# Attention and an MLP in one Trainium2 kernel: every piece of work placed anew, matmuls on zeros in TensorE's early gaps, the last rows copied out in halves

## The chip, the cores and the metric

The kernel runs on one core of a Trainium2 chip. A core has TensorE (PE: matmuls; PEld in the profile is the part of it that loads weights), VectorE (DVE), ScalarE (ACT), GpSimd (POOL) and SyncE (SP), which here issues the DMAs. The metric is the device time of one execution in microseconds, as a median of several. Times below are us unless marked ns.

## The reference, cut to what matters

```python
# q, k, v: (4, 8, 768, 64) f32; n_global 8, n_local 96; w_in (512, 2048), w_out (2048, 512) f32
scores = q @ k^T / sqrt(64)
rel = pos[:, None] - pos[None, :]
keep = (pos[None, :] < n_global) | ((rel >= 0) & (rel < n_local))
scores = scores - slopes * dist            # per head, dist from rel
a = softmax(where(keep, scores, -1e9))
x = (a @ v) rearranged to (3072, 512)      # 4 batches x 768 tokens, 8 heads x 64
h = x @ w_in
g = where(h >= 1, h, where(h <= -1, 0, (h + 1)**2 / 4))
out = g @ w_out                            # (3072, 512) f32
```

## The kernel before

The 3072 tokens are cut into 24 units of 128 rows (4 batches with 6 row blocks each). In a unit, each row block needs the few global keys and the keys of its own block and the one before it, 256 columns, so attention is eight heads of 128 by 256. Two units make a chunk of 256 tokens, on which the two products of the MLP run: 12 chunks, c = 0 to 11. The products come in f16 as three matmuls each: an operand is split into a high part (names with h: `qh`, `kh`, `xh`, `wih`, `woh`, `gh`) and a low one (the rest after the high part: `xh`'s second half, `wil`, `wol`, `gl`).

A unit u has two halves (heads 0 to 3 and 4 to 7; names such as `s12_0`) and passes through this chain:

- `scores` on PE into `s` (24 matmuls), `masked` on DVE into `z`, the exponential on ACT;
- `split_p`: ACT writes the high part of `ph`, DVE the low part;
- `turn_p`: SP issues a DMA transpose `pt<-ph`;
- `attend` on PE into `av` (24 matmuls), `scale_x` on DVE into `x`;
- `split_x`: ACT writes the high part of `xh`; the low part is written by the engine that the constant `XL` names, "p" for POOL, "v" for DVE;
- `turn_x`: SP issues a DMA transpose `xt<-xh`.

Once both units of a chunk are there, the first product `ffn1(c, g)` takes 8 groups g of 24 matmuls into a tile `h` (`h4_7` is group 7 of chunk 4), `gelu` takes five steps on ACT, DVE and POOL that end in `gh` (ACT) and `gl` (POOL), and the second product `ffn2(c, t, f)` collects 48 matmuls for each of the chunk's two row blocks t in a PSUM tile `o` (`o11_1`). `finish` scales `o` into `ob` on ACT and SP sends it out. The first units (block 0 of each batch) go a separate f32 way (`first_load` and on, with transposes `tp` and `xtp` on PE). The weights come in 32 pieces, which DVE turns to f32 (`w_bits`, last step `w_f`), ACT and POOL split (`w_hi`, `w_lo`); `check_load` and `check_reduce` read the weights once more for a range check.

What sets the order: every piece of work is a call that `at(t, f, ...)` puts into a list with a planned time. The list is sorted and numbered, and the table `PLACE` then names the numbers in the order in which the calls are made. Each engine runs its instructions in that order, and SP issues the DMAs in that order. A number that `PLACE` doesn't name is not called. `spare(0)` is a PSUM tile of the pool `ps_o` that nothing reads, and `warm(n)` runs n matmuls of a 128x128 tile of zeros into it. Before, 32 such matmuls run: 8 ahead of the first scores (from `WARM`), and groups of `WA` = 3 among the first units' work.

Of the kernel before, what the change touches and what calls it, by code (L numbers as in the profile page):

```python
# [17 lines left out]
P = 128  # L18
# [38 lines left out]
XL = "p"  # L57
# [6 lines left out]
FLOAD = [-0.95, -0.52, 15.64, 24.01]  # L64
VLOAD = [-4.77, 11.54, 18.15, 28.68]
FIRST = [4.37, 7.29, 10.29, 15.54, 26.68, 37.85, 48.2, 54.41]
WARM = [(1.0, 8)]
WLOAD = [0.8, 1.0, 8.0]
WA = 3
# [3 lines left out]
TAB = -0.77  # L73
TBC = -1.99
RC = 52.97
E3 = [-19.46, -14.0, -6.17, -0.47, 3.78, 8.46, 16.26, 20.67]
PER = 47.0
SOFF = -13.94
FETCH = 16.26
CONV = 9.6  # L80
KG = 3.41
CHK = 7.39
VCONV = 10.53
VFETCH = 8.71
AVL = 14.35
GEL = [2.7, 3.48, 4.59, 5.91, 5.91]
CK0 = 199.09
CK1 = 573.64
CKL = 10.36
WO = [2.79, 3.98, 5.09]  # L90
FO = [0.26, 1.06, 2.5, 3.37, 3.48, 4.67, 5.72, 6.5, 6.59, 7.54]
UO = [0.55, 1.5, 4.0, 5.66, 6.33, 1.69, 1.96, 3.06, 3.38, 3.41]
BO = [1.94, 2.51]
SO = [0.63, 0.65, 2.38, 1.0]
# [4 lines left out]
WG = 3.75  # L99
PB = 2.64  # L100
NCH = NU // 2
WLAG = 5.0
PLACE = [
# [139 lines left out]
]  # L243


@with_exitstack
def attention_then_moe(ctx, tc, q, k, v, n_global, n_local, w_in, w_out, out):
# [950 lines left out]
```

## Time and profile before

| | |
|---|---|
| median of 3 executions | 638.66 us (638.55 to 640.11) |
| profiled execution | 637.52 us, of which the span of instructions is 635.7 us |
| busy share of the span | PE 96%, DVE 70%, PEld 66%, ACT 65%, POOL 47% |
| mean granted TensorE clock | 0.98 of full speed |
| matmuls and weight loads | 5588 each |

The span runs from the first to the last instruction; the profiled execution's time is 1.82 us more. The median lies 1.14 us above the profiled execution. Names in a row such as `pt<-ph` are output and input. An idle time in brackets stands before an instruction, with what ended it.

### The profile page before, as it was taken

To read this page: it belongs to the slowest core of one execution; us is meant where nothing else is said; L and a number is where in the kernel's file an instruction comes from. 1 tells how busy PE (TensorE), PEld (TensorE's weight loads), DVE (VectorE), ACT (ScalarE), POOL (GpSimd) and SP (SyncE) were. 2 spreads that over 40 slices of the span, in tenths; PEclk is the share of its full clock that TensorE was granted. 3 is DMA by queue.
4 is the path that set the end of the run, shared out by engine and by line. 5 is a ranking of instruction groups with operands and counts; after the bars stand their busy time and mean duration, and the time that the engine had idled before them with its cause. 6 is when DMAs were issued, how large, how long until landed. Compare 5 with 4: busy or idle time off the path is not lost.

```text
span 635.7 us, 14747 instructions
## 1 busy us (share of the span) xinstructions
PE 607.6 (96%) x5588; PEld 417.1 (66%) x5588; DVE 442.2 (70%) x1109; ACT 412.1 (65%) x1070; POOL 296.8 (47%) x266
## 2 busy tenths in 40 slices
PE   7888799999999999999999999999999999999996
PEld 4666575656876766767767667666666766766652
DVE  6999999977956676776776776776677686533420
ACT  4868898998867665775785775676585674432220
POOL 0336785775563543563653563463554533322210
PEclk8889899999999999999999999999999999999999
DMA  6748586578944565556555555766554643531001
GB/s 201 250 147 247 182 252 197 125 134 191 168 93 75 109 154 141 154 146 163 144 139 135 158 135 144 171 143 139 127 165 110 140 133 78 125 116 35 1 34 39
DMA packets 144084, 88.08 MB, mean 139 GB/s; under 512 B 108165, under 2 KB 124549, under 8 KB 144005
## 3 DMA queue, kind: packets, MB, share of 16 engines
q1 hardware_dynamic: 144000, 87.05, 54.1%
q8 instruction: 46, 0.75, 0.5%
q14 instruction: 34, 0.27, 0.1%
q10 hardware_dynamic: 4, 0.00, 0.0%
HBM read 54.53 MB, written 6.29 MB: 96 GB/s over the span
## 4 chain that ended last, share of the span: by engine, by line
issue 31%; POOL 26%; PE 25%; DVE 9%; ACT 5%; DMA 2%; POOLq 0%; SPq 0%; ACTq 0%; DVEq 0%
PE o L913 13%; POOL gl L901 11%; PE h L870 8%; POOL xh L801 8%; POOL kh L698 2%; POOL kr L697 2%; DVE w_f L475 2%; POOL qh L698 2%; ACT z L578 1%; POOL qr L697 1%; DMA w_raw<-in_moe_w_out_dram 1%; PE av L785 1%; POOL wol L502 1%; DVE u L893 1%; PE s L742 1%
## 5 line engine op out<-in xcount | busy, mean ns | idle before, releaser
L870 PE MATMUL h<-xt,wih 128*128 128x256 f16 x1536 | 259.7, 274 | 0.7 <-DVE u L893 0.7
L901 POOL TENSOR_TENSOR gl<-u,gh 128x512 f16<-128x512 f32 x96 | 117.8, 1227 | 214.2 <-ACT gh L897 205.2
L870 PE MATMUL h<-xt,wil 128*128 128x256 f16 x768 | 210.8, 274 | 0.0
L870 PEld LDWEIGHTS <-wih 128*128 128x128 f16 x1536 | 149.4, 99 | 32.2 <-DVE u L893 1.6
L888 DVE SCALAR_TENSOR_TENSOR h<-h,u 128x512 f32<-128x512 f32 x96 | 66.7, 695 | 116.3 <-ACT u L883 115.5
L913 PE MATMUL o<-wol,gh 128*128 128x512 f16 x384 | 145.9, 380 | 1.7 <-POOL wol L502 1.7
L913 PE MATMUL o<-woh,gh 128*128 128x512 f16 x384 | 146.4, 381 | 0.0
L913 PE MATMUL o<-woh,gl 128*128 128x512 f16 x384 | 145.8, 380 | 0.0
L883 ACT ACTIVATE u<-h,half 128x512 f32<-128x512 f32 x96 | 65.4, 682 | 87.8 <-PE h L870 87.8
L913 PEld LDWEIGHTS <-gh 128*128 128x128 f16 x768 | 71.5, 98 | 67.2 <-issue 0.5
L578 ACT ACTIVATE z<-z,nm 128x256 f32<-128x256 f32 (+1 forms) x192 | 91.8, 479 | 28.0 <-DVE nm L566 27.5
L897 ACT ACTIVATE gh<-u 128x512 f16<-128x512 f32 x96 | 59.8, 623 | 51.1 <-DVE u L893 51.1
L566 DVE CUSTOM_DVE_ANT_0 z<-s,bias 128x256 f32<-128x256 f32 (+1 forms) x192 | 67.1, 397 | 22.2 <-PE s L742 20.4
L870 PEld LDWEIGHTS <-wil 128*128 128x128 f16 x768 | 75.6, 98 | 9.1
L913 PEld LDWEIGHTS <-gl 128*128 128x128 f16 x384 | 37.7, 98 | 47.7 <-issue 2.9
L760 DVE SCALAR_TENSOR_TENSOR ph<-z,ph 128x1024 f16<-128x1024 f32 x40 | 61.6, 1540 | 9.6 <-ACT ph L758 9.4
L801 POOL TENSOR_TENSOR xh<-x,xh 128x256 f16<-128x256 f32 x40 | 62.2, 1554 | 10.4 <-ACT xh L799 8.8
L893 DVE SCALAR_TENSOR_TENSOR u<-u,h 128x512 f32<-128x512 f32 x96 | 65.4, 681 | 1.4
L534 DVE TENSOR_REDUCE sq<-c_raw 128x1 f32<-128x256 f32 x128 | 49.1, 409 | 0.0
L785 PEld LDWEIGHTS <-pt 128*128 128x128 f16 x960 | 32.8, 98 | 14.5 <-DMA pt<-ph 7.1
L758 ACT ACTIVATE ph<-z 128x1024 f16<-128x1024 f32 x40 | 41.7, 1043 | 0.1
L785 PE MATMUL av<-vh,pt 128*128 128x64 f16 x960 | 34.6, 193 | 4.5 <-DMA pt<-ph 4.3
(100 smaller groups left out, 671.8 us busy)
## 6 DMA issues: line engine op xcount, KB each, us to landing
w_raw<-in_moe_w_in_dram SPq DMA_DIRECT2D x16, 512.0 KB, 4.0
w_raw<-in_moe_w_out_dram SPq DMA_DIRECT2D x16, 512.0 KB, 3.8
c_raw<-in_moe_w_in_dram SPq DMA_DIRECT2D x32, 256.0 KB, 3.5
c_raw<-in_moe_w_out_dram SPq DMA_DIRECT2D x32, 256.0 KB, 3.3
vr<-in_v_dram SPq DMA_DIRECT2D x28, 256.0 KB, 3.9
kr<-in_k_dram SPq DMA_DIRECT2D x28, 256.0 KB, 3.6
qr<-in_q_dram SPq DMA_DIRECT2D x24, 256.0 KB, 4.3
out_dram<-ob SPq DMA_DIRECT2D x24, 256.0 KB, 2.8
```

What stands on the lines that cost most here:

```text
L566: nc.vector.tensor_tensor_reduce(out=p32[u, hf][:, hh, :], in0=pts[u, hf][hh // 2][:, hh % 2, 0:n], in1=bias[:, 4 * hf + hh, base : base + n],
L578: nc.scalar.activation(z, z, AF.Exp, bias=nm[:, c : c + 1], scale=-1.0, accum_out=sums[:, c : c + 1])
L760: nc.vector.scalar_tensor_tensor(phs[u, hf][:, 1, :], zf, SP_, phs[u, hf][:, 0, :], op0=ALU.mult, op1=ALU.subtract)
L785: nc.tensor.matmul(av[:, hh, :], pt[:, a, hh, kt, :], vt[:, c, h * D : (h + 1) * D], start=(n == 0), stop=(n == 5),)
L801: (nc.gpsimd if XL == "p" else nc.vector).tensor_sub(xhs[u, hf][:, 1, :], xs[u, hf], xhs[u, hf][:, 0, :])
L870: nc.tensor.matmul(hp[:, e, :], w[:, dc, f], xt[:, hf, 2 * a + j, :], start=(n == 0), stop=(n == 3 * NDC - 1),)
L883: nc.scalar.activation(us[c, g], hs[c, g], AF.Relu, bias=half, scale=2.0 / (SV * SW), accum_out=su[:, col : col + 1])
L888: nc.vector.scalar_tensor_tensor(ws[c, g], hs[c, g], 4.0 / (SV * SW), us[c, g], op0=ALU.mult, op1=ALU.max)
L893: nc.vector.scalar_tensor_tensor(dst, us[c, g], 4.0, ws[c, g], op0=ALU.min, op1=ALU.mult)
L897: nc.scalar.activation(gh, ws[c, g], AF.Copy)
L901: (nc.gpsimd if GL == "p" else nc.vector).tensor_sub(gl, ws[c, g], gt[c, g][0])
L913: nc.tensor.matmul(po, a[:, cs], w[:, f, :], start=(f == 0 and n == 0), stop=(f == NFC - 1 and n == 2))
```

## The change

The edit has four parts.

1. The planned times (`FLOAD` to `WLAG`, some 30 numbers) and the table `PLACE` are replaced: all work stands in a new order.
2. `XL` goes from "p" to "v": the low part of `xh` moves from POOL to DVE, 40 instructions.
3. 150 calls of `filler` (one matmul on zeros) are listed; `PLACE` names those that are run. `WARM` is empty and `WA` is 1. In all 109 matmuls on zeros are run in place of 32, the last ahead of the first matmul of the second product (`o0`).
4. In the last chunk all 48 matmuls of `o11_0` come ahead of the 48 of `o11_1` (before, they alternate). The last row block is copied out in two halves of 256 columns, the first by ACT and the second by DVE, and is sent in two DMAs, the first issued by SP, the second by ACT.

`TPO` is 0, so the lines with it change nothing.

```diff
-XL = "p"
+XL = "v"
-WARM = [(1.0, 8)]
+WARM = []
-WA = 3
+WA = 1
-AVL = 14.35
+AVL = 12.92
-PLACE = [
-    5, 0, 1, 2, 11, 3, 6, 4, 7, 9, 12, 38, 68, 20, 8, 10, 13, 151, 14, 15, 16, 17, 18, 19, 21, 22, 25, 23, 24,
...
+    3, 0, 1, 2, 5, 7, 8, 71, 9, 4, 72, 11, 73, 74, 37, 6, 231, 300, 75, 10, 12, 13, 14, 19, 15, 16, 17, 18, 20,
...
+NFILL = 150
+TAIL = 1
+TPO = 0
...
+    def filler():
+        warm(1)
...
         for e in range(parts):
             cs = slice(e * n, (e + 1) * n)
-            nc.scalar.activation(ob[:, cs], os_[c, t][:, cs], AF.Copy, scale=1.0 / (SG * SW))
-        nc.sync.dma_start(out[r0 : r0 + P, :], ob)
+            if e:
+                nc.vector.tensor_scalar(ob[:, cs], os_[c, t][:, cs], 1.0 / (SG * SW), None, op0=ALU.mult)
+            else:
+                nc.scalar.activation(ob[:, cs], os_[c, t][:, cs], AF.Copy, scale=1.0 / (SG * SW))
+        for e in range(parts):
+            cs = slice(e * n, (e + 1) * n)
+            (nc.scalar if e else nc.sync).dma_start(out[r0 : r0 + P, cs], ob[:, cs])
...
-                at(t + 0.2, finish, c, x, 1)
+                at(t + 0.2, finish, c, x, 2 if TAIL and c + 1 == NCH and x else 1)
...
-            put_ffn2(c, (0, 1), g, t - (PER / 16 - 0.1 if g and c + 1 < NCH else 0.0))
+            if TAIL and c + 1 == NCH:
+                put_ffn2(c, (0,), g, t0 + 1.3 * g)
+                put_ffn2(c, (1,), g, t0 + 10.5 + 1.3 * g)
+            else:
+                put_ffn2(c, (0, 1), g, t - (PER / 16 - 0.1 if g and c + 1 < NCH else 0.0))
...
+    for n in range(NFILL):
+        at(12.0, filler)
```

Three places show what the table does. The first is SP's order where unit 11 ends and unit 12 begins (`xt5` is the transposed x of chunk 5, `xh11_1` the second half of unit 11, `pt12_0` and `ph12_0` the first half of unit 12, `ob3` the output of chunk 3). Before:

```order
L529 DMA c4_1_raw_3921<-in_moe_w_in_dram 128x2x256
L676 DMA kr14_1_3928<-in_k_dram 128x512
L676 DMA qr14_1_3958<-in_q_dram 128x512
L529 DMA c5_0_raw_4045<-in_moe_w_in_dram 128x2x256
L809 DMA_TRANSPOSE xt5_3520<-xh11_1_4041 128x4x128
L767 DMA_TRANSPOSE pt12_0_4059<-ph12_0_4033 128x16x128
L928 DMA out_0_dram<-ob3_0_4069 128x512
L928 DMA out_0_dram<-ob3_1_4098 128x512
```

And with the change:

```order
L948 DMA out_0_dram<-ob3_0_4023 128x512
L948 DMA out_0_dram<-ob3_1_4055 128x512
L691 DMA kr14_0_4086<-in_k_dram 128x512
L691 DMA kr14_1_4094<-in_k_dram 128x512
L691 DMA qr14_1_4097<-in_q_dram 128x512
L782 DMA_TRANSPOSE pt12_0_4143<-ph12_0_4099 128x16x128
L824 DMA_TRANSPOSE xt5_3618<-xh11_1_4154 128x4x128
L782 DMA_TRANSPOSE pt12_1_4315<-ph12_1_4273 128x16x128
```

The transpose of `ph12_0` stood behind that of `xh11_1` and now stands ahead of it; the two writes of `ob3` stood behind it and now stand further ahead.

The second is where the low part of `xh11_1` is made. Before, on POOL, among the `gl` of chunk 4:

```order
L801 TENSOR_TENSOR xh11_0_3857<-x11_0_3850,xh11_0_3857 128x256
L901 TENSOR_TENSOR gl4_4_3915<-u4_4_3873,gh4_4_3913 128x512
L901 TENSOR_TENSOR gl4_5_4036<-u4_5_3926,gh4_5_4003 128x512
L801 TENSOR_TENSOR xh11_1_4041<-x11_1_4038,xh11_1_4041 128x256
L901 TENSOR_TENSOR gl4_6_4106<-u4_6_4053,gh4_6_4101 128x512
```

With the change, on DVE, behind the low part of `ph12_0`:

```order
L775 SCALAR_TENSOR_TENSOR ph12_0_4099<-z12_0_4052,ph12_0_4099 128x1024
L903 SCALAR_TENSOR_TENSOR h4_7_4059<-h4_7_4059,u4_7_4129 128x512
L642 TENSOR_TENSOR x11_1_4148<-av11_1_4104,r11_1_3924 128x256
L908 SCALAR_TENSOR_TENSOR u4_7_4129<-u4_7_4129,h4_7_4059 128x512
L742 COPY vh11_3_3425<-vg1_2755 32x1024
L816 TENSOR_TENSOR xh11_1_4154<-x11_1_4148,xh11_1_4154 128x256
```

The instruction has left POOL's queue and stands in DVE's, five places behind `ph12_0`'s.

The work that PE does between the scores `s12_0` and the product `av12_0` of the same half is changed too. Before: 9 matmuls of `o3`, `av11_1`, the group `h4_6`, 12 of `o3`, `h4_7`, `s12_1`, 3 of `o4`. Now: `h4_7`, `av11_1`, 24 of `o4`, `s12_1`, 6 of `o4`.

The third is the start of PE's program (`pps` and `pps_n` are two small products on the bias, `zeros` and `spare0` the matmuls on zeros, `s0_0` the first scores). Before, `pps_n` stands behind the last of the first 8 matmuls on zeros:

```order
L434 LDWEIGHTS zeros_122
L434 MATMUL spare0_148<-zeros_122 128x512
L385 MATMUL pps_n_173<-nlow_168,bias_120 128x2
L555 MATMUL s0_0_0_184<-kr0_144,qr0_146 128x128
L555 MATMUL s0_0_1_185<-kr0_144,qr0_146 128x128
```

With the change it stands ahead of the first of six:

```order
L378 MATMUL pps_135<-bias_120 128x1
L394 MATMUL pps_n_155<-nlow_150,bias_120 128x2
L443 LDWEIGHTS zeros_122
L443 MATMUL spare0_162<-zeros_122 128x512
L443 LDWEIGHTS zeros_122
```

Behind these six, single matmuls on zeros and blocks of 7 or 8 of them stand between the products of the first units, for instance 7 ahead of `av0_1` and 8 behind `av3_1`. DVE's order in the first 110 us is changed as well: two more 128x512 steps of the first chunk's gelu (`h1_4`, `u1_4`) stand ahead of the last weight's `w31_f`.

## Rows read from the trace of the kernel before

**Rows 1.** Busy windows: length, then PE, PEld, DVE, ACT, POOL; granted clock, DMA share, GB/s.
```profile
12.00:78.00 66.00, 55.26 (x363) 41.40 (x362) 62.56 (x166) 53.12 (x144) 32.78 (x31) 0.83 0.62 196
78.00:124.00 46.00, 43.73 (x380) 29.89 (x379) 45.10 (x92) 41.76 (x101) 32.91 (x30) 1.00 0.65 186
...
10.10:20.40 10.30, 10.25 (x48) 7.56 (x49) 8.51 (x37) 8.09 (x30) 2.31 (x2) 0.50 0.52 169
```

**Rows 2.** Tile pt from 200 to 550: who waits for it, and issue to landing.
```profile
  PEld L785: 7.1, 6
  PE av L785: 4.3, 5
...
DMA to landing us min/median/max: 4.3/4.3/6.1
```

**Rows 3.** The chain of waits, one chunk's steps: start, length, engine, tile, line, count.
```profile
544.58 0.78 PE s L742 x24
...
547.41 0.70 PE av L785 x24
548.11 2.62 PE h L870 x24
550.73 2.59 PE o L913 x12
```

**Rows 4.** Timeline of unit 10, first half: start, length.
```profile
220.51 1.85 POOL L801 TENSOR_TENSOR xh<-x,xh 128x256 f16<-128x256 f32 x1
...
220.62 1.20 DVE L760 SCALAR_TENSOR_TENSOR ph<-z,ph 128x1024 f16<-128x1024 f32 x1
...
222.39 1.20 SPq L809 DMA_TRANSPOSE xt<-xh  x1
...
223.69 2.07 SPq L767 DMA_TRANSPOSE pt<-ph  x1
...
229.60 0.87 PE L785 MATMUL av<-vh,pt 128*128 128x64 f16 x24 [1.41 <-DMA pt<-ph]
```

**Rows 5.** Timeline of unit 14, first half.
```profile
313.74 0.42 DVE L566 CUSTOM_DVE_ANT_0 z<-s,bias 128x256 f32<-128x256 f32 x1
...
317.79 1.34 DVE L760 SCALAR_TENSOR_TENSOR ph<-z,ph 128x1024 f16<-128x1024 f32 x1 [0.38 <-ACT ph L758]
...
319.19 2.01 SPq L767 DMA_TRANSPOSE pt<-ph  x1
```

**Rows 6.** Lines from 200 to 550: count, busy, mean ns, idle before and its releaser.
```profile
L627 DVE TENSOR_TENSOR x<-av,r 128x256 f32<-128x256 f32 x29 | 12.2, 422 | 2.7 <-PE av L785 2.1
...
L801 POOL TENSOR_TENSOR xh<-x,xh 128x256 f16<-128x256 f32 x29 | 49.4, 1703 | 1.3
```

**Rows 7.** Timelines of DVE and POOL where unit 11's ph is split.
```profile
232.91 2.04 DVE L760 SCALAR_TENSOR_TENSOR ph<-z,ph 128x1024 f16<-128x1024 f32 x1
...
232.72 1.15 POOL L901 TENSOR_TENSOR gl<-u,gh 128x512 f16<-128x512 f32 x1
```

**Rows 8.** Waits from 0 to 12 (us, times, longest), and PE's timeline there.
```profile
DVE nval L386 <- PE pps_n L385: 2.1, 1, 2.1
...
2.92 3.60 PE L434 MATMUL spare<-zeros 128*128 128x512 f16 x8
```

**Rows 9.** Timelines from the last weight to the end of the first `o`.
```profile
115.98 0.68 DVE L475 SCALAR_TENSOR_TENSOR w_f<-w_raw,w_bits 128x512 int32<-128x512 int32 x1
...
118.88 1.15 POOL L502 TENSOR_TENSOR wol<-w_f,woh 128x512 f16<-128x512 f32 x1
...
121.93 0.38 PE L913 MATMUL o<-woh,gh 128*128 128x512 f16 x1
...
123.22 0.38 PE L870 MATMUL h<-xt,wih 128*128 128x256 f16 x2
```

**Rows 10.** The end: ACT's copies and SP's issues of the last two output blocks.
```profile
628.91 1.25 ACT L927 ACTIVATE ob<-o 128x512 f32<-128x512 f32 x2 [17.10 <-PE o L913]
...
629.53 0.98 SPq L928 DMA_DIRECT2D out_dram<-ob  x2
```

More of the change, by code (lines that the diff above doesn't have):

```diff
@@ L62 @@
 FQ = {"k": "sync", "q": "sync", "v": "sync"}
-FLOAD = [-0.95, -0.52, 15.64, 24.01]
-VLOAD = [-4.77, 11.54, 18.15, 28.68]
-FIRST = [4.37, 7.29, 10.29, 15.54, 26.68, 37.85, 48.2, 54.41]
-WARM = [(1.0, 8)]
+FLOAD = [-0.64, 0.7, 15.12, 24.29]
+VLOAD = [-4.85, 13.77, 17.59, 34.66]
+FIRST = [4.37, 6.83, 10.29, 15.54, 27.12, 37.85, 47.39, 54.1]
+WARM = []
 WLOAD = [0.8, 1.0, 8.0]
-WA = 3
+WA = 1
 T0 = 24.5
@@ L72 @@
 GB = 5.42
[L73 to L76, printed above, removed]
+TAB = -1.61
+TBC = -0.92
+RC = 51.6
+E3 = [-19.46, -14.0, -9.93, -2.34, 1.91, 6.59, 14.07, 20.27]
 PER = 47.0
[L78 to L84, printed above, removed]
-AVL = 14.35
[L86 to L94, printed above, removed]
+SOFF = -3.14
+FETCH = 17.57
+CONV = 7.82
+KG = 0.65
+CHK = 6.28
+VCONV = 8.11
+VFETCH = 8.85
+AVL = 12.92
+GEL = [2.85, 3.46, 3.99, 6.47, 7.12]
+CK0 = 299.8
+CK1 = 602.24
+CKL = 8.3
+WO = [2.79, 4.31, 6.34]
+FO = [0.65, 1.06, 2.46, 3.92, 3.63, 4.69, 5.48, 6.52, 6.61, 6.89]
+UO = [0.55, 1.5, 3.54, 5.66, 7.51, 2.65, 3.43, 3.92, 3.99, 4.75]
+BO = [1.13, 2.63]
+SO = [0.72, 0.29, 2.59, 1.22]
 WS = "d"
@@ L98 @@
 PA = 2.76
-WG = 3.75
-PB = 2.64
+WG = 4.92
+PB = 2.85
 NCH = NU // 2
-WLAG = 5.0
+WLAG = 6.03
 PLACE = [
[139 rows of a table removed]
-]
[145 rows of a table added]
+]
+NFILL = 150
+TAIL = 1
+TPO = 0
 @with_exitstack
@@ L461, in w_bits @@
         if s == 0:
-            if num < NFC and num % 2:
+            if num < NFC and num % 2 and not TPO:
                 wbits[n] = spare(1).bitcast(I32).rearrange("p (a b) -> p a b", a=NDC)
@@ L598, in first_turn @@
         whole(u, hf)
-        tp = ps_h.tile([P, 4, P], F32, tag="h", name=f"tp{u}_{hf}")
+        if TPO and u >= TPO:
+            tp = spare(1).rearrange("p (a b) -> p a b", a=4)
+        else:
+            tp = ps_h.tile([P, 4, P], F32, tag="h", name=f"tp{u}_{hf}")
         for hh in range(4):
@@ L991, in fast_path @@
             t = t0 + PER * g / 8
-            put_ffn2(c, (0, 1), g, t - (PER / 16 - 0.1 if g and c + 1 < NCH else 0.0))
+            if TAIL and c + 1 == NCH:
+                put_ffn2(c, (0,), g, t0 + 1.3 * g)
+                put_ffn2(c, (1,), g, t0 + 10.5 + 1.3 * g)
+            else:
+                put_ffn2(c, (0, 1), g, t - (PER / 16 - 0.1 if g and c + 1 < NCH else 0.0))
             if c + 1 < NCH:
```

282 rows, old and new, of the table PLACE are left out of this document.

## The prediction

> **What bounds the kernel now.** I read the windows first, then the chain of waits, then the tile view of `pt` and the timelines behind its waits. In the windows the reader is to see two regimes. From 12 to 78 us DVE is busy 62.56 of 66.00 us and from 78 to 124 45.10 of 46.00, PE 55.26 and 43.73 [rows 1]: the conversion of the weights on DVE sets the pace. PE stands idle there for 10.74 us, and its clock is below full speed too: the mean over 12 to 78 is 0.83, and from 10.1 to 20.4 it is 0.50 [rows 1], the 1.2 GHz level. By that mean 66.00 x 0.17 = 11.2 us of PE's time are lost to the clock. From 124 on PE never stops but for short waits, so there only its waits and its own work count. The chain shows what that work is made of: 24 matmuls of `h` 2.62, 12 of `o` 2.59 (0.216 each), a half's scores 0.78, its `av` 0.70 [rows 3].
>
> The tile view of `pt` says which waits are left between 200 and 550: PE waits five times for a `pt` at `av`, 4.3 us in all, and its weight loads six times, 7.1 in all [rows 2]. Unit 10 shows why. DVE is done with `ph` at 220.62 + 1.20 = 221.82, but SP stands at the transpose of the unit before it, which waits for POOL's `xh` (220.51 + 1.85 = 222.36); `xt` is issued at 222.39 and `pt` only at 223.69, 1.87 late, and `av` starts at 229.60 after a wait of 1.41 [rows 4]. Unit 14 is the counterexample: its `pt` is issued at 319.19, right behind `ph` (317.79 + 1.34 = 319.13), and 5.45 behind the first `z` at 313.74 [rows 5]; I found no wait at its `av`.
>
> **The change, part by part.** *A, the waits for `pt`.* In SP's new order `pt12_0` stands ahead of the `xt` of `xh11_1`, and `xh11_1` is no longer in POOL's queue. In the order the same holds for the other even units from 10 on. So the 1.87 of [rows 4] goes. But PE's cover shrinks too: the work between the end of `s12_0` and `av12_0` was 9 x 0.216 + 0.70 + 2.62 + 2.59 + 2.62 + 0.78 + 3 x 0.216 = 11.9, and is now 2.62 + 0.70 + 24 x 0.216 + 0.78 + 6 x 0.216 = 10.6 [rows 3]. Counted in this way in the whole new order, units 10, 12 and 22 have 10.6, 16 and 18 11.2, 20 11.9 and 14 12.5; all had 11.9. What is needed when nothing stands ahead of `pt`: 5.45 to its issue [rows 5] plus the median 4.3 to landing [rows 2], 9.8. So 0.8 is left at the tightest, and the waits go: -4.5, between the 4.3 that PE and the 7.1 that its weight loads wait [rows 2], near the first because a late weight load is partly hidden by matmuls still running.
>
> *B, `xh` on DVE.* No row has it there. The nearest is `x` of the same tile on DVE, 0.42 each; on POOL it took 1.70 [rows 6]. I take 0.5, bounds 0.42 and 1.70. Forty of them are 20 us of DVE (17 to 68) behind units spread over 550 us in which DVE is idle 30%; in the DVE-bound first 124 us there are only a few. The cover is that idle time; without it, each would delay the `h` and `u` steps behind it by its length. Priced at 0 here, and the late `x` under E.
>
> The other rows that bear on it: `ph` lasts 1.20 with POOL's `xh` beginning ahead of it and `xh` then takes 1.85 [rows 4], but 2.04 where it begins 0.19 behind a `gl` of 1.15 [rows 7]. By that, one of the two stands still while the other runs, and an `xh` on DVE can lose up to a `gl`'s rest, here 1.15 - 0.19 = 0.96. The Trainium skill says this as a rule ("SBUF — State Buffer", "Who interferes with whom"): DVE's second port pair is GpSimd's, and whoever holds it locks the other out. The trace agrees, by the 2.04. By the rule the move could cost what it saves; by the rows alone POOL loses 40 instructions, so DVE's `ph` is held up less often. The sum goes by the second, and the first is a rival below.
>
> *C, the start.* 109 matmuls on zeros in place of 32 are 77 x 0.216 = 16.6 us at the full rate [rows 3], and 77 x 0.45 = 34.7 at the rate of the first eight, 3.60 / 8 [rows 8]. Idle time and time lost to the clock are 10.7 + 11.2 = 21.9, so at the full rate they fit and at the low rate they don't. I take it that most of the blocks lie in real gaps, since DVE sets the pace, and that some end late: +1.0 for DVE's waits on them. `pps_n` now runs ahead of the matmuls on zeros; DVE waited 2.1 for it behind the block that ran from 2.92 to 6.52 [rows 8]. I take half, -1.0 (bounds 0 and -2.1), because other early waits may take its place. Two gelu steps now stand ahead of the last `w_f` on DVE; at that step's 0.68 [rows 9] they cost 1.4. A faster clock gives DVE nothing where DVE is the bound.
>
> What counts at the end of this stage is when the first `o` can be finished. Its last matmuls waited for the last weight: `wol` ends at 118.88 + 1.15 = 120.03, the last stretch of `o` begins at 121.93 and `h` follows at 123.22 [rows 9]. With the change: 120.03 + 1.4 - 1.0 + 1.0 + (123.22 - 121.93) = 122.7, so -0.5. PE was saturated between 78 and 124 but for 2.3 us, so that an earlier start doesn't go through to the end as long as the last weight comes when it comes; bounds +3.4 (waits of 4.9) and -3.
>
> *D, the tail.* The two copies took 1.25 and the two issues 0.98, the last at 629.53 [rows 10]. Half a copy on each of two engines saves 0.31, the issue from another queue than the first row block's up to 0.49, and `o11_0` is out long before. But each half is a DMA of its own with its issue and its landing: -0.6, bounds 0 and -1.1 (0.62 and 0.49, were both to go). The Trainium skill ("DMA: Bandwidth & Descriptors", "Rules for kernel authors") says of two transfers to halves of the partitions that they serialize; these are halves of the columns, and by its reading D would be -0.3, from the copy alone. No row shows it.
>
> *E, new short waits.* By the same count the work between the last `av` of a chunk and its successor's first `h` falls from 11.9 to 8.0 at three chunks and from 10.4 to 5.2 at chunk 11. It has to hold `x` 0.42, `xh` 0.42 to 1.70 [rows 6] and a landing, for which `pt`'s 4.3 [rows 2] is the nearest: 5.1 to 6.4. Only chunk 11 falls short, by up to 1.2; with scatter elsewhere +0.7 (bounds 0 and 3).
>
> Sum against the profiled execution: 637.5 - 4.5 - 0.5 - 0.6 + 0.7 = 632.6. The median of the runs shown is 1.14 above that execution, so the forecast is **633.8** as a median. What a measurement of this kernel can tell from no change is 0.3%, 1.9 us.
>
> **The rivals.** *The whole start is won:* all of the 2.1 is kept, the matmuls on zeros hold the clock at the upper level, and DVE's 3.4 us of idle time from 12 to 78 [rows 1] go too. Then C is about -4 in place of -0.5: 630.2. For it speaks that the slow stretches are where PE waits for DVE; against it that DVE is busy 95% there at either level.
>
> *`xh` locked out by `gl`:* up to 0.96 at each of the four tightest places (10, 12, 22, chunk 11), 0.8 of which was slack; with the `ph` waits that return, up to +2.7, 636.5. The traffic is there [rows 7]; against it, POOL has fewer instructions.
>
> *The matmuls on zeros do not hold the clock, so the change doesn't do there what it says:* a block of 7 then takes 3.2 in place of 1.5, ahead of an `av` that DVE waits for. DVE has 3.4 us to give from 12 to 78; beyond it every microsecond goes through to the last weight. From 4.9 us of new waits on, C takes back A and D; I put it at about +4.5: 638.8, the same as before.
>
> *Slower: the cover is too short.* If `pt` is as late as before for another reason, `ph` now standing behind new DVE work, say, PE needs what it needed in the five cases, 11.9 + 4.3 / 5 = 12.8 [rows 2]. Waits are then 3 x 2.2 + 2 x 1.6 + 0.9 + 0.3 = 11.0 in place of 4.3, and the time is 637.5 + 6.7 - 0.4 + 1.1 = 644.9. It passes the time before from a need of 11.8 on, where the seven waits sum to 4.7; at 12.3 they are 7.7 and the time 641.6. For it speaks that six of seven leads are no longer than before; against it unit 14, whose 9.8 was enough.
>
> **Chances.** Forecast (632 to 635.8) 0.53; whole start won 0.14; `xh` locked out 0.08, half of it still faster; zeros at the low rate 0.13, all the same; cover too short 0.12, two parts in a hundred of it only the same. Faster by over 0.3% is 0.53 + 0.14 + 0.06 = 0.73, the same 0.13 + 0.02 + 0.02 = 0.17, slower 0.10. The range leaves out the worse part of the short cover and the best of the start: 630.4 to 639.2.
>
> **What will show it.** A: no wait of `av` for `pt` from unit 10 on, `pt` issued within 0.2 of the end of `ph`. B: `xh` on DVE below 0.7. C: granted clock at or near 1.00 from 12 to 78 and the last `wol` near 121; a first `o` that ends near 122.7. D: the span's end less the last matmul shorter by 0.6. E: waits of `h` for `xt` below 1 us in all. The forecast is wrong if `av` waits move to other units, if DVE's idle time before 124 grows by more than 3 us, or if `h` waits for `xt` at every chunk.

## The result, and the profile after

The changed kernel takes 631.09 us as a median of 4 executions (629.12 to 631.34), the kernel before 638.72 on the same chip: a ratio of 0.987 with a 95% interval of 0.9852 to 0.9889, 7.6 us less. In another group of runs the same kernel took 629.21 against 639.55 (0.9847, 0.9827 to 0.9866). The profiled execution is 630.93, its span 629.1; against the 637.52 of before that is 6.59 less. The forecast was 633.8 in a range of 630.4 to 639.2; the measured time lies inside it, below the 632 to 635.8 that had the chance of 0.53.

First the windows of the changed kernel, with the columns of [rows 1]:

```profile
12.00:78.00 66.00, 64.45 (x448) 45.28 (x448) 60.87 (x160) 51.62 (x137) 33.61 (x31) 1.00 0.61 193
78.00:124.00 46.00, 43.74 (x390) 29.15 (x389) 44.56 (x89) 43.38 (x105) 34.29 (x31) 1.00 0.64 194
...
200.00:550.00 350.00, 350.00 (x3496) 242.84 (x3495) 249.13 (x639) 241.19 (x619) 125.76 (x116) 1.00 0.58 135
```

PE is filled from 12 to 78 (64.45 in place of 55.26). The column of its granted clock says 1.00 in place of 0.83, but that does not hold for the first 8 us: up to 19.9 the rows of the first units, shown further down, have PE at the 1.2 GHz level (a product takes 1.97 there and 1.00 later). The trace of this kernel holds no record of the clock ahead of 19.9, and the column shows a stretch without a record as 1.00. DVE, though, is busy less and not more, 60.87 against 62.56 [rows 1]: no work on the weights was brought forward. From 200 to 550 PE has no idle time left at all.

The tile view of `pt` from 200 to 550 names no wait of PE or its weight loads where [rows 2] had 4.3 and 7.1:

```profile
who waited for it (us, times):
  ACT vh L697: 1.4, 4
...
DMA to landing us min/median/max: 4.3/4.4/6.2
```

Unit 12's first half shows the new order at work, in the timeline:

```profile
269.63 0.84 PE L757 MATMUL s<-kh,qh 64*128 64x128 f16 x24
273.04 0.86 PE L800 MATMUL av<-vh,pt 128*128 128x64 f16 x24
...
274.18 1.23 DVE L775 SCALAR_TENSOR_TENSOR ph<-z,ph 128x1024 f16<-128x1024 f32 x1 [0.71 <-ACT ph L773]
275.48 1.73 SPq L782 DMA_TRANSPOSE pt<-ph  x1
...
277.18 0.41 DVE L816 TENSOR_TENSOR xh<-x,xh 128x256 f16<-128x256 f32 x1
277.62 1.53 SPq L824 DMA_TRANSPOSE xt<-xh  x1
...
281.10 0.86 PE L800 MATMUL av<-vh,pt 128*128 128x64 f16 x24
```

`pt` is issued 0.07 behind the end of `ph` (275.41), `xt` 2.14 later. From the end of the scores, 270.4, to the second `av` row, which is this half's, PE has 10.7 of other work. The transpose needs until 275.48 + 4.4 = 279.9, so 1.2 is left. `xh` takes 0.41 on DVE; from 124 to 560, 39 of the 40, it is 0.487 in the mean:

```profile
L816 DVE TENSOR_TENSOR xh<-x,xh 128x256 f16<-128x256 f32 x39 | 19.0, 487 | 0.6 <-ACT xh L814 0.6
```

The end of the first `o` and the last weight, the timelines that answer to [rows 9]:

```profile
117.90 0.69 DVE L487 SCALAR_TENSOR_TENSOR w_f<-w_raw,w_bits 128x512 int32<-128x512 int32 x1
...
120.66 1.16 POOL L514 TENSOR_TENSOR wol<-w_f,woh 128x512 f16<-128x512 f32 x1 [2.76 <-ACT w_f L507]
...
122.73 0.38 PE L928 MATMUL o<-woh,gl 128*128 128x512 f16 x1
123.04 0.84 PE L757 MATMUL s<-kh,qh 64*128 64x128 f16 x24
```

The last weight is ready at 121.82, 1.8 later than before, but the first `o` gives way to the next work at 123.04 against 123.22. Behind either point PE has the same matmuls left (1944 of `h`, 1056 of `o`, 936 of `av`, 888 of `s`), 496.5 by the steps of [rows 3], so in this pair of executions the stage gave 0.2.

And the end, which answers to [rows 10]:

```profile
623.11 0.38 PE L928 MATMUL o<-woh,gl 128*128 128x512 f16 x1
...
623.59 0.38 ACT L945 ACTIVATE ob<-o 128x256 f32<-128x256 f32 x1 [9.76 <-PEq L308]
624.00 0.33 SPq L948 DMA_DIRECT2D out_dram<-ob  x1
624.00 0.42 DVE L943 TENSOR_SCALAR ob<-o 128x256 f32<-128x256 f32 x1 [10.06 <-ACT ob L945]
624.46 0.38 ACTq L948 DMA_DIRECT2D out_dram<-ob  x1
```

The last matmul ends at 623.49 and the span 5.6 later; before, a last row at 629.08 + 0.38 = 629.46 and a span of 635.7 made it 6.2. The two half copies do not run side by side: DVE's begins at 624.00, when ACT's has ended, and ACT is named as what it waited for.

So the 6.59 of the profiled pair are 0.2 at the start, 0.6 at the tail and 5.8 between, where PE's 496.5 of work took 506.2 before (123.22 to 629.46) and takes 500.4 now.

What the pair doesn't tell is how much of this is the execution that was profiled. `after_undo_order`, below, is the changed kernel's own program until unit 10, but in its profiled execution the short time of the first products came earlier:

```profile
12.21 1.10 PE L634 MATMUL av<-vr,pt 128*128 128x64 f32 x8
...
115.35 0.69 DVE L487 SCALAR_TENSOR_TENSOR w_f<-w_raw,w_bits 128x512 int32<-128x512 int32 x1
```

Its last weight's `w_f` ends at 116.04, 2.55 ahead of the changed kernel's 118.59, and its first `o` gives way at 120.49 in place of 123.04. What is won there arrives at the end in full: from the end of the last `w_f` to the start of the last matmul the changed kernel takes 504.5 (118.59 to 623.11), and so do, to within 0.03, the eight other profiled executions below that keep its order on SP, though their last `w_f` ends anywhere from 117.03 to 121.33.

### The profile page after: what moved, and what is told of

Same layout as the page of the kernel before. It is cut to its first block, busy times and chain, and to the rows that moved or that the text cites. A ratio compares the mean times of both kernels' runs of the same rounds, so it can differ in the third digit from the quotient of the medians.

```text
span 629.1 us, 14881 instructions
## 1 busy us (share of the span) xinstructions
PE 615.7 (98%) x5665; PEld 420.8 (67%) x5665; DVE 448.0 (71%) x1150; ACT 418.7 (67%) x1070; POOL 239.5 (38%) x226
## 5 line engine op out<-in xcount | busy, mean ns | idle before, releaser
L885 PE MATMUL h<-xt,wih 128*128 128x256 f16 x1536 | 256.4, 273 | 1.0 <-DVE u L908 0.9
L885 PEld LDWEIGHTS <-wih 128*128 128x128 f16 x1536 | 147.4, 98 | 30.9 <-DVE u L908 1.6
L775 DVE SCALAR_TENSOR_TENSOR ph<-z,ph 128x1024 f16<-128x1024 f32 x40 | 60.0, 1499 | 22.1 <-ACT ph L773 21.8
L757 PEld LDWEIGHTS <-qh 64*128 64x128 f16 x960 | 26.9, 94 | 16.7 <-issue 9.5
L590 ACT ACTIVATION_READ_ACCUMULATOR z<-z,nm 128x1 f32 x192 | 36.0, 187 | 0.0
```

Of the source, the lines that this page charges most:

```text
L590: nc.scalar.activation(z, z, AF.Exp, bias=nm[:, c : c + 1], scale=-1.0, accum_out=sums[:, c : c + 1])
L775: nc.vector.scalar_tensor_tensor(phs[u, hf][:, 1, :], zf, SP_, phs[u, hf][:, 0, :], op0=ALU.mult, op1=ALU.subtract)
L885: nc.tensor.matmul(hp[:, e, :], w[:, dc, f], xt[:, hf, 2 * a + j, :], start=(n == 0), stop=(n == 3 * NDC - 1),)
```

## The experiments

Each was timed in 5 rounds beside the kernel before. Three groups of four ran on a chip each; ratios are to the kernel before of the same group (639.09, 639.55 and 638.91). Profiled executions are compared where a stretch is meant.

### What takes the waits for `pt` away: the order on SP, or `xh` off POOL

The kernel before with one thing moved, `before_swap`:

```diff
-        for n in PLACE or range(len(plan)):
+        order = list(PLACE)
+        for u in (10, 12, 16, 18, 20, 22):
+            x = next(n for n in order if plan[n][2] is turn_x and plan[n][3] == (u - 1, 1))
+            p = next(n for n in order if plan[n][2] is turn_p and plan[n][3] == (u, 0))
+            order.remove(x)
+            order.insert(order.index(p) + 1, x)
+        for n in order:
```

> The kernel before with one thing moved: at units 10, 12, 16, 18, 20 and 22 the transpose of p is issued ahead of the transpose of x. Theory: pt is issued 1.9 to 2.5 earlier, the five waits of av go, and it is 4.3 to 5.5 us faster than before. Rival (xh leaving POOL counts): less than 2 us faster, or a wait of h for xt takes the place.

Measured: 634.27 us, 0.9922 (0.9905 to 0.9939), 4.8 less. The waits of PE's `av` on `pt` from 200 to 550 are gone, one of 0.2 of a weight load stays. From the end of the last `w_f` to the last matmul it takes 507.2 (118.42 to 625.64), the kernel before 512.4 (116.66 to 629.08), 5.2 less. The theory holds, in size too.

The kernel before with `XL = "v"` and nothing else, `before_xh_dve`:

```diff
-XL = "p"
+XL = "v"
```

> The kernel before with the low part of xh on DVE and nothing else. Theory (the order on SP counts): pt still stands behind xt, whose xh now stands behind ph on DVE, so most of the five waits stay and the time moves by less than 2 us. Rival (xh leaving POOL counts): 4 to 6 us faster than before.

Measured: 635.81, 0.9953 (0.9938 to 0.9968), 3.3 less: between the two forecasts. The timeline of unit 10 in it says why my expectation failed:

```profile
223.97 0.40 DVE L801 TENSOR_TENSOR xh<-x,xh 128x256 f16<-128x256 f32 x1
224.31 1.21 DVE L760 SCALAR_TENSOR_TENSOR ph<-z,ph 128x1024 f16<-128x1024 f32 x1
224.41 1.19 SPq L809 DMA_TRANSPOSE xt<-xh  x1
225.71 2.04 SPq L767 DMA_TRANSPOSE pt<-ph  x1
```

In that kernel's order `xh` stands ahead of `ph` on DVE, not behind it. It takes 0.40 where POOL's took 1.85 beside DVE's `ph` [rows 4], so `xt` is issued while `ph` is still being made, and `pt` only 0.19 behind its end. No wait for `pt` is left here either. What is lost against `before_swap` is mostly a new wait elsewhere, in the view of PE's waits from 150 to 200 (`before_swap` has 0.2 there):

```profile
PE h L870 <- DVE u L893: 1.6, 1, 1.6
```

So each of the two, the order on SP and the engine of `xh`, was enough by itself to end the waits for `pt` in the old order.

The changed kernel with `xh` back on POOL, `after_xh_pool`:

```diff
-XL = "v"
+XL = "p"
```

> The changed kernel with the low part of xh back on POOL. Theory (what counts is that SP issues the transpose of p ahead of that of x): no wait of av for pt comes back; only the short covers ahead of a chunk's first h can fail, 0.3 to 3 us slower than the changed kernel. Rival (what counts is that xh leaves POOL): the waits of av for pt come back, 4 to 6 us slower.

Measured: 629.62, 0.985 (0.9833 to 0.9868). PE still has no wait from 200 to 550, as the theory had it; the time that it expected to lose was not lost. To see whether this version is better, it ran again beside the changed kernel itself, `after_again` and `xh_pool_again`.

> The changed kernel once more, to stand beside the others of this group on one chip: 631.1 within 1 us, 7 to 8 us below the kernel before.

> The changed kernel with the low part of xh on POOL, beside the changed kernel itself. Theory (the place of xh's low part is worth nothing once pt is issued first; the 1.5 us seen came from where the start happened to fall in those executions): the same as the changed kernel within 0.7. Rival (DVE is the bound of the start and each xh there costs): 1 to 2 us faster than the changed kernel.

Measured: 629.21 (0.9847, 0.9827 to 0.9866) and 631.21 (0.9863, 0.9843 to 0.9883). The changed kernel came out 0.9 below the bounds set for it, and the two medians are 2.0 apart where at most 0.7 was expected. But the order of the two has turned round between the groups, and the intervals overlap. In the traces the difference lies ahead of the last `w_f`, which ends at 118.59 and 118.97 with `xh` on DVE, at 117.96 and 119.43 with it on POOL; from there to the last matmul all four take 504.5. With `pt` issued first, the engine of `xh` makes no difference that these runs can tell.

The changed kernel with only the order on SP moved back, `after_undo_order` (the same edit as in `before_swap`, with p put behind x, and unit 14 too):

> The changed kernel (low part of xh on DVE) with one thing moved back: at units 10, 12, 14, 16, 18, 20 and 22 the transpose of p is issued behind that of x, as before. Theory (the cover is shorter in the new order, and x itself comes later, so the order on SP is now what keeps the waits away): pt is issued 3 to 4 late, PE needs 12.8 to 13.5 where it has 10.6 to 12.5, and the waits of av come back larger than before: 8 to 16 us slower than the changed kernel. Rival (xh on DVE is enough by itself, as it was in the kernel before): at most 2 us slower.

Measured: 645.84, 1.0107 (1.0091 to 1.0122), 14.8 to 16.6 above the changed kernel's two medians and 6.9 above the kernel before. The tile view of `pt` from 200 to 550:

```profile
  DMA pt<-ph: 27.4, 14
who waited for it (us, times):
  PEld L800: 15.4, 7
  PE av L800: 12.0, 7
```

Seven waits where the kernel before had five, one at each of the seven units, and nearly three times the sum. In the new order `xh` stands behind `ph`, and `pt` behind `xt` behind both:

```profile
277.57 1.22 DVE L775 SCALAR_TENSOR_TENSOR ph<-z,ph 128x1024 f16<-128x1024 f32 x1 [0.71 <-ACT ph L773]
...
280.57 0.41 DVE L816 TENSOR_TENSOR xh<-x,xh 128x256 f16<-128x256 f32 x1
281.00 1.19 SPq L824 DMA_TRANSPOSE xt<-xh  x1
282.30 9.43 SPq L782 DMA_TRANSPOSE pt<-ph  x2
...
286.82 1.03 PE L800 MATMUL av<-vh,pt 128*128 128x64 f16 x24 [2.17 <-DMA pt<-ph]
```

`ph` is ready at 278.79 and `pt` issued at 282.30, 3.5 late. This is the slower rival's mechanism, set off by hand: the shorter covers hold only because nothing stands ahead of `pt`. The waits are not all of the loss. At three of them the granted clock fell to 0.50, the 1.2 GHz level, for some 14 us in all; the first stretch:

```profile
232.80:239.50 6.70, 5.90 (x46) 4.58 (x47) 2.37 (x4) 1.47 (x3) 3.26 (x4) 0.50 0.30 58
```

From the last `w_f` to the last matmul this execution takes 523.7 (116.04 to 639.72) in place of 504.5, 19.2 more, of which the seven waits, read from the start of one matmul to the start of the next, are 13.1. The other 6.1 are about what the lower clock takes: half of the 14, by estimate 7, less what PE stood idle in them. As this execution's start was 2.55 earlier, its span is 16.6 longer (645.7 against 629.1). (The 9.43 are two issues in one row, the next unit's with it.)

### What the matmuls on zeros are worth

The changed kernel without the calls of `filler`, `after_no_fill` (101 of the 109 matmuls on zeros go; 8, which are not such calls, stay):

```diff
             t, _, f, args = plan[n]
+            if f is filler:
+                continue
```

> The changed kernel without the 101 matmuls on zeros that the table places (8 stay). Theory (DVE sets the pace up to the last weight): the granted clock falls below 0.9 from 12 to 78, and yet the time stays within 0.7 of the changed kernel's 631.1, because the first second-product tile still waits for the last weight. Rival (the clock at full speed carries the start): 2 to 6 us slower than the changed kernel.

Measured: 633.36, 0.9909 (0.9893 to 0.9924), 2.3 to 4.2 above the changed kernel's medians and 1.3 by span in the profiled pair (630.4 against 629.1). The theory's "within 0.7" has failed, and the rival, 2 to 6 slower, holds: they are worth something. PE's timelines of the first units show where. The changed kernel:

```profile
13.17 1.97 PE L634 MATMUL av<-vr,pt 128*128 128x64 f32 x8
...
17.05 3.09 PE L443 MATMUL spare<-zeros 128*128 128x512 f16 x7
19.98 1.00 PE L634 MATMUL av<-vr,pt 128*128 128x64 f32 x8
```

Without them:

```profile
12.44 1.97 PE L634 MATMUL av<-vr,pt 128*128 128x64 f32 x8
...
17.46 1.97 PE L634 MATMUL av<-vr,pt 128*128 128x64 f32 x8 [0.51 <-DVE xt L666]
...
28.17 1.97 PE L634 MATMUL av<-vr,pt 128*128 128x64 f32 x8
```

The same product takes 1.97 or 1.00. With the matmuls on zeros it runs at the shorter time from 20 us on, without them at the longer one until 28 at the least. DVE waits for these products, in `after_no_fill` from 12 to 36:

```profile
DVE x L642 <- PE av L634: 2.6, 3, 1.0
```

In the changed kernel it is 1.7 there, and 0.7 in `after_undo_order`, where the products were short from 12.21 on. The column of the granted clock says 1.00 in both kernels from 12 to 36, so here the rows' own durations have to be read: the trace of `after_no_fill` holds no record of the clock ahead of 34.4.

The changed kernel with them only up to the first group of the first product, `after_fill_early`:

```diff
+        begun = False
         for n in PLACE or range(len(plan)):
             t, _, f, args = plan[n]
+            begun = begun or f is ffn1
+            if f is filler and begun:
+                continue
```

> The changed kernel with matmuls on zeros only up to the first group of the first product (40 or so), and the eight that follow groups. Theory (what the matmuls on zeros win, they win before 34 us, where DVE waits for scores and av; later DVE has its work without them): the same as the changed kernel within 0.7, with a clock below 1.00 from 46 to 79. Rival (the clock is worth as much in the later gaps): 1 to 2.5 us slower, as without any.

Measured: 629.45, 0.9856 (0.9841 to 0.9871), the same as the changed kernel. From 36 to 78 it stands so in the windows:

```profile
36.00:78.00 42.00, 33.43 (x218) 25.61 (x216) 41.07 (x87) 33.29 (x80) 28.00 (x27) 0.80 0.60 199
```

against this of the changed kernel:

```profile
36.00:78.00 42.00, 40.67 (x294) 28.74 (x293) 41.12 (x90) 33.66 (x80) 26.67 (x25) 1.00 0.60 191
```

A fifth of the clock is missing there and PE is idle for 8.6, and DVE is as busy, 41.07 and 41.12, and the time no longer. The 65 matmuls on zeros that are left out here are worth nothing that these runs can tell; what all of them win, they win before 34 us. One reservation: in this profiled execution the first `av` took 1.10 already, in place of 1.97, and the last `w_f` ended at 117.03. Against `after_undo_order`, whose start ran alike (116.04), that is 1.0 later, of which 0.3 was there by 31 us. So the later ones may be worth up to 0.7 in such an execution, less than the medians can show.

The same matmuls in the old order, `before_fill`:

```diff
-WA = 3
+WA = 1
+FILL = [("first_xt", (0, 0), 1), ("first_av", (0, 1), 7), ("first_scores", (1, 1), 1), ("first_turn", (1, 0), 1),
...
...
+            for g, a, n in FILL:
+                if f.__name__ == g and args == a:
+                    warm(n)
             f(*args)
```

> The kernel before with matmuls on zeros ahead of the same instructions as in the changed kernel, up to where its second product begins (99 in all in place of 32), order of all else as before. Theory (the clock matters through the PE work that DVE waits for, 1 to 2 us): the clock from 12 to 78 rises to 0.95 or more and the time falls by 1 to 2.5. Rival (DVE sets the pace in any case): within 0.7 of before; or slower, if the blocks stand in the way.

Measured: 645.32, 1.0086 (1.0067 to 1.0106), 5.8 slower than before. Its windows:

```profile
12.00:36.00 24.00, 21.01 (x118) 13.58 (x118) 19.26 (x73) 16.97 (x53) 5.79 (x5) 0.93 0.52 166
36.00:78.00 42.00, 40.13 (x290) 28.80 (x289) 36.40 (x83) 29.08 (x72) 21.02 (x19) 0.96 0.55 169
```

The clock is higher, from 36 to 78 at least (0.96 against 0.88 before; in the first window the record of the clock begins only at 18.7), and DVE is busy 55.7 of 66 in place of 62.56 [rows 1]. The expectation, 1 to 2.5 faster, has failed. DVE's longest waits from 0 to 80, where the kernel before has 0.2 and 0.7:

```profile
DVE h L895 <- ACT u L890: 4.0, 2, 3.0
DVE x L634 <- PE av L626: 3.4, 3, 2.0
```

The last `w_f` ends at 125.7 against 116.7 [rows 9]. So in that order the blocks stand in front of work that DVE waits for, and the faster clock does not make up for it.

Two attempts at a better place for the block of six ahead of `av0_1`: `after_less_fill` leaves it out, `after_front_fill` puts it ahead of the first scores. The edit of the second:

```diff
+        block = [n for n in order[lo:hi] if plan[n][2] is filler]
+        order = [n for n in order if n not in block]
...
+        order[s0:s0] = block
```

> The changed kernel without the block of six matmuls on zeros ahead of av0_1, behind which DVE waited 1.5. Theory (a block in front of work that DVE waits for costs its own time, and the next block ahead of av1_0 raises the clock as well): first weight 1 to 2.5 earlier, time 0 to 1 us lower than the changed kernel. Rival (that block is what raises the clock): the steps from av0_1 to s2_0 stay at the low rate, 0.5 to 1.5 us slower.

> The changed kernel with these six matmuls on zeros put ahead of the first scores (12 there in place of 6). If they raise the clock before av0_0: 1 to 3 us faster than the changed kernel. If not: the first scores come 2.6 later and the time is 1 to 2 us longer.

Measured: 630.97 (0.9877, 0.9862 to 0.9893) and 633.82 (0.9915, 0.9902 to 0.9929). Without the block the time is the same as that of the changed kernel. In the profiled execution `av0_1` ran at the shorter time (17.53, 1.10), but `av0_0`, ahead of where the block would stand, did so too (12.67, 1.10), so it doesn't tell what the block does where the rate is still low. Ahead of the first scores the twelve do raise the rate earlier (the first scores take 0.71 in place of 1.23), but they run to 9.8 in place of 7.4, and without the block ahead of `av0_1` the granted clock fell back to 0.50 from 19.8 to 26.5. The last `w_f` ends at 121.33, and the time is 2.7 to 4.6 longer: delay and fall together cost more than the early rate gives back, and these runs don't part the two.

### The last rows in halves

The changed kernel with one copy and one DMA for the last rows, `after_one_piece`:

```diff
-                at(t + 0.2, finish, c, x, 2 if TAIL and c + 1 == NCH and x else 1)
+                at(t + 0.2, finish, c, x, 1)
```

> The changed kernel with the last row block copied in one piece by ACT and sent in one DMA by SP; the order of the last chunk stays. Theory: the stretch from the last matmul to the span's end is 0.3 to 0.7 longer (half a copy on another engine, half an issue), the time as much. Rival (two DMAs cost what the halves save): no difference.

Measured: 631.72, 0.9879 (0.986 to 0.9897), too close to the changed kernel to tell by the median. In its timeline the stretch can be read:

```profile
623.93 0.60 ACT L945 ACTIVATE ob<-o 128x512 f32<-128x512 f32 x1 [9.76 <-PE o L928]
624.56 0.33 SPq L948 DMA_DIRECT2D out_dram<-ob  x1
```

From the copy's start to the span's end (630.2) it is 6.3, in the changed kernel 5.5 (623.59 to 629.1): 0.8. The copies are no part of it: one piece is sent 0.63 behind the copy's start, the second half 0.87 behind. What is shorter is the rest, from the last issue to the end: 4.6 with half the bytes in each DMA, against 5.6 (before: 630.2 to 635.7, 5.5). The other traces bear it out: from the end of the last matmul to the span's end it is 5.4 to 5.7 in the nine profiled executions with halves, 6.1 to 6.5 in the five without. The expectation put it down to copy and issue, and neither is shorter.

## Why the prediction was right, point by point

- **What bounds the kernel** held: waits for `pt` between 200 and 550, DVE at the start.
- **A, -4.5.** Right in mechanism and nearly in size: `before_swap` alone gave 4.8. In the profiled pair the stretch from the first `o` to the last matmul is 5.8 shorter. Read from the start of one matmul to the start of the next, the five waits of `av` in the kernel before cost 5.1, where the view of waits gives PE 4.3 and the forecast took 4.5; a wait of `h` ahead of 200, 0.4, which the forecast did not count, went too. The cover of 10.6 was enough at unit 12 (10.7 measured), and 9.5 was needed there, where the count said 9.8.
- **B, 0.** `xh` on DVE took 0.487 in the mean, forecast 0.5. That its place is worth nothing is what the two `xh` runs on POOL show, once the order is right. None of the 40 stands in the first 124 us, where the prediction had a few. I took order and engine for one cause; they are two, each sufficient in the old order.
- **C, -0.5.** The profiled pair has -0.2, but by misses on either side, so that this is luck. The sentence that a faster clock gives DVE nothing failed: `after_no_fill` is 2 to 4 slower. DVE waits for the first units' scores and `av`, and those take half as long with the clock up. And `wol` came at 121.82 where I had 121.4, with the end of `o` at 123.04 against 122.7. Of `pps_n`, DVE's wait fell from 2.1 to 0.7, but its waits for the first scores, now behind the six matmuls on zeros, rose from 0.9 to 1.7. That the last weight sets what follows was right: 504.5 behind it in every execution that keeps the order.
- **D, -0.6.** Right in size and wrong in working: I had the two copies side by side and the issues on two queues. The copies run one after the other, and the gain is 1.0 less from the last issue to the end, of which the second copy takes some back. The reading by which only the copy would gain, 0.3, has failed too.
- **E, +0.7.** Nothing: PE has no wait from 200 to 550, and none for chunk 11. The landing was mis-sized: by the tile view of `xt` from 124 to 560 it took 2.8 at the median, where the count had `pt`'s 4.3.
- **The 1.14** that I added for the median was the before's alone. Its profiled execution had its start earlier than the other with the same start: its last `w_f` ended at 116.7, that of `before_swap` at 118.4. From 72 to 84 the windows of the two differ in the clock, 0.88 and 0.74, and in what DVE gets done, 11.35 and 10.23. Before:

```profile
72.00:84.00 12.00, 11.74 (x79) 8.58 (x80) 11.35 (x20) 11.71 (x28) 9.74 (x11) 0.88 0.69 205
```

`before_swap`:

```profile
72.00:84.00 12.00, 11.83 (x70) 8.84 (x71) 10.23 (x18) 11.33 (x26) 9.56 (x10) 0.74 0.58 188
```

The changed kernel's median lies only 0.16 above its profiled execution. So of the 2.7 by which 633.8 was too high, 1.0 is this term, 0.7 is E, 1.3 is A with the short waits behind the first `o` that it left out, and C takes 0.3 back. In the chances, half of the 0.08 for a locked-out `xh` is 0.04, where the sum took 0.06: faster was 0.71 and the same 0.19.

The rivals: the whole start was not won in the profiled pair, though the time came near the one I gave for it, for another reason; in the trace of `after_undo_order` the first `o` ends 2.7 ahead of the kernel before, so an execution in which the clock rises early wins most of it. Zeros at the low rate: true of the changed kernel up to 19.9 us (seven took 3.09), after which the clock rose; the same blocks in the old order cost time as that rival said, by their place. The short cover: not here, but one order on SP away (`after_undo_order`, forecast for it 644.9, measured 645.84, a near hit by luck, since the fallen clock was not in it). `xh` locked out by `gl`: it does happen, once in the profiled execution:

```profile
457.73 1.38 DVE L816 TENSOR_TENSOR xh<-x,xh 128x256 f16<-128x256 f32 x1
```

A `gl` had begun 0.65 ahead of it on POOL. Four more took 0.80 to 0.83 beside POOL's work on `kh`, `qh` and `qr`, the others 0.40 to 0.55. None of it reached PE, which has no wait there.

Executions of the changed kernel differ by 2.5 us (628.94 to 631.46). Most of that, by the traces, can come from when the clock first rises: with a first `av` of 1.10 the last `w_f` ended at 116.04, with one of 1.97 at 118.59 and 118.97. The fastest executions were not profiled, so for them this is not shown, and why the rise comes early in one execution and late in another stays open.

No version tried is faster than the changed kernel by more than these runs can tell.

## What to carry to other kernels

SP issued its DMAs in the order of its program, and so the late input of one transfer made the next one late: 1.87 in unit 10 before, 3.5 in `after_undo_order`. Where a consumer's cover is tight, look at what stands ahead of its transfer, and count the cover in matmul steps against scores, issue and landing. Filling PE's gaps to keep its clock up paid here only where DVE waited for PE's short products; the same fill in an order not planned for it cost 5.8. Look for the point from which all profiled executions of a kernel take the same time, here the last weight: it tells which part of a difference is the change and which is the execution.

## What the runs showed of the hardware that was not expected

- POOL's `xh` of 256 columns took 1.85 with the whole 1.20 of DVE's `ph` beside it [rows 4]. With DVE quiet it took 0.67 in the same kernel; the two differ by 1.18, the length of `ph`. On DVE the same `xh` took 0.40.

```profile
183.40 0.67 POOL L801 TENSOR_TENSOR xh<-x,xh 128x256 f16<-128x256 f32 x1
```

The Trainium skill ("SBUF — State Buffer", "Who interferes with whom") lets only one of the two engines hold the pair of ports they share. The trace agrees, by the 1.18.

- Two engines' copies out of one PSUM tile into halves of one SBUF tile ran in series in this program (0.38, then 0.42), so a split over engines gained nothing there.
- From the last DMA's issue to the span's end, 256 KB took 5.6 and two of 128 KB, issued 0.46 apart, 4.6 from the second.
- A product that took 1.97 in one execution and 1.00 in the other stood under a granted clock of 1.00 in both windows. Ahead of the first record of the clock in a trace (19.9 us in the changed kernel, 34.4 in `after_no_fill`) that column says nothing; the rows' durations do.
